# Half of a Fourier stage from the other half by symmetry, a third PSUM bank for the MLP, and two banks in turn for the first value products

## The chip, the cores and the metric

The kernel runs on one core of a Trainium2 chip. The metric is the device time of one execution in microseconds (us); the time before is the median of three runs. A profile is one execution taken by the hardware profiler. PE is TensorE, DVE is VectorE, ACT is ScalarE, POOL is GpSimd, SP is SyncE, which here only issues DMAs. SBUF is the on-chip memory, PSUM the banks that PE writes its sums into.

## The reference

Chunked attention with a few memory keys, then a Fourier mixing layer with an MLP, on 4 batches, 8 heads, 768 positions and 64 values per head (so 512 columns):

```python
for c in range(nc):                       # chunks of 32 queries
    k_full = concat([mem_k, k[l_start:r_end]])      # 8 memory keys, 16 left, 8 right of the chunk
    a = softmax(scale * q_c @ k_full.T)
    out[:, :, c_start:c_end] = a @ v_full
x = out.transpose(0, 2, 1, 3).reshape(B, S, 512)
mixed = real(fft(fft(x, axis=1), axis=2))
u = x + mixed
un = (u - mean(u)) / sqrt(var(u) + 1e-06)           # over the 512 columns
result = u + maximum(un @ w_ch1, 0) @ w_ch2         # 512 -> 2048 -> 512
```

For real x, the real part of the two-dimensional transform at position S - k and column 512 - c is that at position k and column c.

## The kernel before

Work is written as tasks (`add(engine, cost, emit, after, take, give)`) with an engine, an estimated cost, predecessors and the buffers that a task takes and gives. `Plan.order` runs a list schedule over the estimates, and the instructions are emitted in that order. On the chip, each engine works through its own list in order and waits on semaphores for the others. So a task that is late holds everything behind it on its engine.

**Attention** works on pairs of heads, n = 0 to 15, four to a batch. POOL loads q and k (`e_load_qk`, L286), SP loads v with the memory values (`e_load_v`, L295 to L304). PE turns q and k by transposes (trq and trk, L313); ACT or DVE copies them (qT, kT). PE makes the scores of six tiles of 64 queries at a time (g = 0 and 1; `e_scores`, sc, L351) into a bank of its own, ACT takes the exponential (`e_exp`, L359), and PE multiplies with the values (`e_values`, L372) into the one bank xa. DVE divides by the sums and stores the result as rows of x in SBUF (`e_norm`, L382 and L383; tile `xsb`, 6 tiles of 128 positions by 512 columns).

**Fourier stage.** DVE folds x by symmetry over columns and positions (zy, pq, ff; L400 to L417, in batch 0 by parts, L468 to L486), ACT and DVE split it into two fp16 parts (`e_hi`, `e_lo`, in batch 0 `g_hi`, `g_lo`), and PE transforms over positions (`e_rows`, ps, L440; in batch 0 `g_rows`, L534). ACT and DVE split the result into two fp16 parts (`e_up`, L452; `e_rest`, L456). par = 0 and 1 are the even and odd halves of the columns, ab = 0 and 1 the cosine and sine parts. Only 385 of the 768 positions are computed; DVE writes the mirrored ones as a reversed copy (`e_dn`, L461). Then PE transforms over columns for each of the six tiles (`e_columns`, pm, L545, eight matmuls of 256 columns): tiles 0 to 2 from up, tiles 3 to 5 from dn. DVE adds x (`e_sum`, L551) and takes mean and variance (`e_stats`), ACT subtracts the mean (`e_un`, L563). The result is transposed for the MLP, in batch 0 by PE (tp, L570, and `e_unT`), in the others by a DMA that SP issues (`e_flip`, L575).

**MLP.** For each half of a batch (three tiles): 16 times four matmuls into ph (L596), each followed by ACT's relu into hT (L603); then three tiles of 16 matmuls into pc (L610), each followed by DVE's scaling and addition (`e_osb`, L616) and ACT's output DMA (`e_out`, L620). MLP matmuls are fillers: they go where PE has nothing more urgent. Eight halves follow one another, in order of batches.

**PSUM.** Two banks `acc` hold trk (batch 0), ps and pm; two banks `mlp` hold ps for par = 1 of batch 0, tp, ph and pc; sc, tr and xa have one each. In the last batch alone every third ph or pc takes acc:

```python
def mtag(b, i):
    return "acc" if b == B - 1 and i % 3 == 2 else "mlp"
```

Up to the first ps, the plan puts matmuls on zeros (`e_fill`, L654) into PE's gaps, into one of the mlp banks.

DMAs of SP and ACT signal on eight semaphores in turn, in the order of emission; a DMA waits until the one before it on its semaphore has landed.

Of the kernel before, what the change touches and what calls it, by code (L numbers as in the profile page):

```python
# [10 lines left out]
FP32 = mybir.dt.float32  # L11
BF16 = mybir.dt.bfloat16
FP16 = mybir.dt.float16
AFT = mybir.ActivationFunctionType
ALU = mybir.AluOpType
# [16 lines left out]
def strided(src, off, dims):  # L32
    return bass.AP(tensor=src.tensor, offset=src.offset + off,
                   ap=[list(src.ap[0])] + [list(d) for d in dims])
# [105 lines left out]
def kernel(  # L140
# [51 lines left out]
    plan = Plan(dict(qs=NS, ks=NS, va=NV, kTb=NKT, qT=2, tr=1, sc=1, xa=1, e1=3,  # L192
                     xsb=3, fold=2, hl=1, up=4, dn=4, acc=2, mlp=2, un=6, unT=2, hT=1, osb=3))
    add = plan.add
# [168 lines left out]
    def e_values(n, g):  # L363
        e1 = e1_of.pop((n, g))
        xa = aps.tile([P, 3, 2, 66], FP32, tag="xa", bufs=1, name="xa")
        xa_of[n, g] = xa
        for st in range(3):
            for hh in range(2):
                v1 = va[n % NV]
                for half in range(2):  # L370
                    t6 = 2 * st + half
                    nc.tensor.matmul(xa[64 * half:64 * half + 64, st, hh, 0:65],  # L372
                                     e1[:, hh, t6, :], v1[:, hh, 6 * g + t6, 0:65],
                                     start=True, stop=True)
# [13 lines left out]

    zy_of, pq_of, ff_of, hl_of, ps_of, up_of, pm_of, un_of, tp_of = ({} for _ in range(9))
    mu_of, unT_of, rstd_of, g_of = {}, {}, {}, {}  # L390
    mid = cpool.tile([P, 2, NST, 1], FP16)
    mid32 = cpool.tile([P, NST, 1], FP32)
    warm = cpool.tile([P, 1], FP32)
    gate = cpool.tile([P, 1], FP32)

# [63 lines left out]
    def e_dn(b, par, ab):  # L459
        dn = fpool.tile([P, 2, HS], FP16, tag="dn", bufs=4, name="dn")  # L460
        nc.vector.tensor_copy(dn, rev_ap(up_of[b, par, ab][2], HS, HS, [[2 * NK, 2]]))  # L461
        up_of[b, par, ab][1] = dn

    def g_zy(par, g):
# [84 lines left out]
    def e_sum(b, kt):  # L549
        uv = xs[b][:, kt, :].rearrange("p (j c) -> p c j", c=2)  # L550
        nc.vector.tensor_tensor(uv, pm_of.pop((b, kt)), uv, ALU.add)  # L551

# [19 lines left out]
    def e_flip(b, kt):  # L572
        if kt == 0:
            unT_of[b] = fpool.tile([P, NDT, S], FP16, tag="unT", bufs=2, name="unT")
        nc.sync.dma_start_transpose(unT_of[b][:, :, ts(kt, P)], un_of.pop((b, kt)))  # L575

# [9 lines left out]


    def mtag(b, i):
        return "acc" if b == B - 1 and i % 3 == 2 else "mlp"

# [22 lines left out]
    def e_osb(b, sh, stl):  # L613
        st = sh * 3 + stl
        osb_of[b, st] = osb = fpool.tile([P, DM], FP32, tag="osb", bufs=3, name="osb")
        nc.vector.scalar_tensor_tensor(osb, pc_of.pop((b, sh, stl)), rstd_of[b][:, st:st + 1],  # L616
                                       xs[b][:, st, :], ALU.mult, ALU.add)

    def e_out(b, st):
        nc.scalar.dma_start(out[b, ts(st, P), :], osb_of.pop((b, st)))  # L620


    t_zero = add("DVE", 0.2, e_zero, rank=-21)
# [68 lines left out]
    def attention(n):  # L692
# [25 lines left out]
        for g in range(2):  # L718
            s_ = add("PE", 0.32, lambda g=g: e_scores(n, g), [eq, ek], take=("sc",),
                     give=("qT", "kTb") if g == 1 else ())  # L720
            t_sc[n, g] = s_
            x_ = add("ACT", 2.4 if (n, g) == (0, 0) else 1.12, lambda g=g: e_exp(n, g),
                     [s_, t_masks, t_after.get(n)], take=("e1",), give=("sc",))
            tag = "xa"
            v_ = add("PE", 0.85, lambda g=g: e_values(n, g), [x_, lv, t_low[n % NV]], take=(tag,),
                     rank=len(plan.tasks) + (50 if (n, g) == (2, 1) else 25) if first else None,
                     give=("e1", "va") if g == 1 else ("e1",))
            take = ("xsb",) if g == 0 and n % HP == 0 else ()
            t_norm[n, g] = add("DVE", 0.78, lambda g=g: e_norm(n, g),
                               [v_, t_norm[n - n % HP, 0] if (n % HP, g) != (0, 0) else None],  # L730
                               take=take,
                               give=(tag,))
# [61 lines left out]
    def first_fourier():  # L794
# [38 lines left out]
        return columns_of(0, t_rest)  # L833

    def fourier(b):
        nrm = [[t_norm[b * HP + i, g] for i in ii for g in range(2)] for ii in ((0, 1), (2, 3))]
        t_rest = {}
# [27 lines left out]
    def columns_of(b, t_rest):  # L865
        t_dn = {}
        for par in range(2):
            for ab in range(2):
                t_dn[par, ab] = add("DVE", 0.36, lambda par=par, ab=ab: e_dn(b, par, ab),
                                    [t_rest[par, ab]], take=("dn",))  # L870
        t_un = {}
        allr = list(t_rest.values())
        cols = {}

        def columns(kt):
            cols[kt] = add("PE", 0.9, lambda: e_columns(b, kt),
                           allr + [t_rows] + (list(t_dn.values()) if kt > 2 else []),
                           take=("acc",), rank=len(plan.tasks) + (15 if kt == 3 else 0),
                           give=("up",) * 4 if kt == 2 else ("dn",) * 4 if kt == 5 else ())

        sa = None
        columns(0)
        for kt in range(NST):
            if kt + 1 < NST:
                columns(kt + 1)
            su = add("DVE", 0.7, lambda kt=kt: e_sum(b, kt), [cols[kt]], give=("acc",))
            sa = add("DVE", 0.9, lambda kt=kt: e_stats(b, kt), [su, sa])
            un = add("ACT", 0.72, lambda kt=kt: e_un(b, kt), [sa], take=("un",))
            if b > 0:
                t_un[kt] = add("SP", 0.1, lambda kt=kt: e_flip(b, kt), [un, t_un.get(kt - 1)],  # L890
                               take=("unT",) if kt == 0 else (), give=("un",), moved=0.8,
                               loose=True)
                continue
# [9 lines left out]
    def mlp(b, t_un, rs):  # L903
        for sh in range(2):
            relu = []
            c2 = None
            for ht in range(NHT):
                ph = add("PE", 0.65, lambda sh=sh, ht=ht: e_ch1(b, sh, ht),
                         mlp_prev + [t_un[3 * sh + i] for i in range(3)] + t_w1,
                         take=(mtag(b, ht),), give=("unT",) if sh == 1 and ht == NHT - 1 else (),  # L910
# [5 lines left out]
            for stl in range(3):  # L916
                st = 3 * sh + stl
                for part in range(4):
# [6 lines left out]
                          take=("osb",),   # L925
                          give=(mtag(b, stl), "xsb") if st == NST - 1 else (mtag(b, stl),),
                          rank=RELU(len(plan.tasks)))
                mlp_prev[0] = c2
                add("ACT", 0.1, lambda st=st: e_out(b, st), [os_], give=("osb",), moved=0.9,
                    rank=RELU(len(plan.tasks)))  # L930
# [47 lines left out]
```

## Time and profile before

| | us |
|---|---|
| median of three runs (308.47 to 309.29) | 309.03 |
| the profiled execution's own time | 308.85 |
| its span, first to last instruction | 307.1 |
| PE / DVE / ACT / POOL busy | 289.5 / 171.2 / 161.5 / 40.8 |
| first matmul that is kept (trq) | 6.47 |
| first ps of batch 0 | 42.4 |
| MLP of batch 0 begins | 65.1 |
| last matmul ends | 303.15 |

The span is 1.75 us shorter than the execution's time. Matmuls overlap in PE's pipeline, so what one costs is the distance to the next one's start, not its own duration. The chain of waits is followed back from the last instruction; what it names is what the end hung on. A wait that ends on "issue" hung on nothing that the profile shows.

### The profile page before, as it was taken

What the parts mean: (1) busy time and instruction counts of PE and PEld (TensorE: products, weight loads), DVE (VectorE), ACT (ScalarE), POOL (GpSimd) and SP (SyncE); (2) the same over time, 40 slices, a digit from 0 to 9 for tenths busy, and PEclk for the clock granted to TensorE, in tenths of its full rate; (3) what the DMA queues carried; (4) which work ended last, traced back from release to release, by engine and by line L of the source; (5) the groups of instructions that cost most, each with busy time, mean ns of one, the idle gap of its engine ahead of it and who ended that gap; (6) DMA issues with size and microseconds to landing.
All of it is one profiled execution on the core that took longest, in us unless ns stands there. A gap on an engine that the chain in (4) does not pass through costs nothing.

```text
span 307.1 us, 7496 instructions
## 1 busy us (share of the span) xinstructions
PE 289.5 (94%) x3148; PEld 181.5 (59%) x3148; DVE 171.2 (56%) x371; ACT 161.5 (53%) x291; POOL 40.8 (13%) x78
## 2 busy tenths in 40 slices
PE   1399999999999999999989999999999999999994
PEld 1267678866666676666756646675554554554541
DVE  7877895975397887797764399476101001001001
ACT  6656373689884666885257423743360450531710
POOL 8806421132201102000020000000200000000000
PEclk9999999999999999999999999999999999999999
DMA  6989999999944925821361011004201101001011
GB/s 114 197 171 167 204 205 196 198 204 178 193 72 91 203 45 111 136 47 40 89 137 36 2 46 59 0 19 102 86 2 40 64 2 68 34 2 71 31 36 68
DMA packets 60289, 28.93 MB, mean 94 GB/s; under 512 B 48480, under 2 KB 56672, under 8 KB 60256
## 3 DMA queue, kind: packets, MB, share of 16 engines
q1 hardware_dynamic: 47168, 11.61, 21.0%
q0 software_dynamic: 9344, 10.49, 20.8%
q10 hardware_dynamic: 3744, 6.36, 5.7%
q8 instruction: 25, 0.41, 0.5%
q14 instruction: 8, 0.07, 0.1%
HBM read 30.28 MB, written 6.29 MB: 119 GB/s over the span
## 4 chain that ended last, share of the span: by engine, by line
PE 91%; DMA 2%; POOL 2%; DVE 1%; ACT 1%; issue 1%; POOLq 0%; ACTq 0%
PE ph L596 28%; PE pc L610 27%; PE xa L372 9%; PE pm L545 7%; PE ps L440 5%; PE idle L654 5%; PE ps L534 4%; PE sc L351 3%; DMA qs<-in_q_dram 2%; PE trk L313 2%; PE trq L313 2%; DVE osb L616 1%; POOL qs L286 0%; ACT hT L603 0%; PE tp L570 0%
## 5 line engine op out<-in xcount | busy, mean ns | idle before, releaser
L603 ACT ACTIVATE hT<-ph 128x384 f16<-128x384 f32 x128 | 60.9, 492 | 63.0 <-PE ph L596 51.5
L596 PE MATMUL ph<-unT,w_sb 128*128 128x384 f16 x512 | 91.6, 326 | 2.2 <-ACT hT L603 1.1
L610 PE MATMUL pc<-w_sb,hT 128*128 128x512 f16 x384 | 86.9, 379 | 0.0
L596 PEld LDWEIGHTS <-w_sb 128*128 128x128 f16 x512 | 47.8, 97 | 36.8 <-issue 5.7
L616 DVE SCALAR_TENSOR_TENSOR osb<-pc,rstd,xsb 128x512 f32<-128x512 f32 x24 | 18.0, 749 | 82.5 <-PE pc L610 82.4
L610 PEld LDWEIGHTS <-hT 128*128 128x128 f16 x384 | 36.8, 98 | 41.2 <-issue 0.2
L359 ACT ACTIVATE e<-sc,mbias 128x384 f32<-128x384 f32 x64 | 33.8, 583 | 13.8 <-PE sc L351 11.3
L372 PEld LDWEIGHTS xa<-va,e 128*64 128x64 f32 x768 | 25.0, 137 | 7.8 <-issue 7.0
L372 PE MATMUL xa<-va,e 128*64 128x65 f32 x768 | 29.3, 226 | 0.0
L563 ACT ACTIVATE un<-xsb,mu_s 128x512 f16<-128x512 f32 x24 | 17.2, 720 | 14.9 <-DVE mu_s L558 14.8
L382 DVE RECIPROCAL zs<-xa 128x6 f32<-128x6 f32 x32 | 6.1, 191 | 25.6 <-PE xa L372 25.5
L452 ACT CAST up<-ps 128x386 f16<-128x386 f32 x16 | 9.7, 603 | 19.1 <-PE ps L440 13.5
L551 DVE TENSOR_TENSOR xsb<-pm,xsb 128x512 f32<-128x512 f32 x24 | 16.0, 675 | 4.4 <-PE pm L545 4.2
L383 DVE TENSOR_TENSOR xsb<-xa,zs 128x384 f32<-128x384 f32 x32 | 17.8, 557 | 1.1
L557 DVE BATCH_NORM_STATS2 st<-xsb 128x6 f32<-128x512 f32 x24 | 16.4, 684 | 0.5
L654 PE MATMUL idle<-dz 128*128 128x384 bf16 x71 | 15.3, 350 | 1.0 <-DVE zero L230 1.0
L322 ACT COPY qT<-trq 128x768 bf16<-128x768 bf16 x16 | 12.8, 798 | 5.6 <-PE trq L313 5.5
L286 POOL DMA_DIRECT2D ks<-in_k_dram x16 | 10.2, 635 | 35.0 <-PE trk L313 31.4
L584 POOL TENSOR_SCALAR rstd<-mu_s 128x6 f32<-128x6 f32 x4 | 1.0, 245 | 102.0 <-DVE osb L616 57.7
L313 PE MATMUL trq<-ident_b,qs 96*64 96x96 bf16 x256 | 9.4, 221 | 5.1 <-DMA qs<-in_q_dram 5.1
L286 POOL DMA_DIRECT2D qs<-in_q_dram x16 | 10.5, 659 | 25.2 <-PE trq L313 21.5
L456 DVE TENSOR_TENSOR up<-ps,up 128x386 f16<-128x386 f32 x16 | 9.6, 598 | 7.5 <-ACT up L452 7.5
(126 smaller groups left out, 343.5 us busy)
## 6 DMA issues: line engine op xcount, KB each, us to landing
va<-in_v_dram SPq DMA_DIRECT2D x32, 220.0 KB
out_dram<-osb ACTq DMA_DIRECT2D x24, 256.0 KB
w_sb<-in_moe_w_ch_dram POOLq DMA_DIRECT2D x8, 512.0 KB, 16.9
qs<-in_q_dram POOLq DMA_DIRECT2D x16, 192.0 KB, 5.7
ks<-in_k_dram POOLq DMA_DIRECT2D x16, 192.0 KB, 6.1
va<-in_mem_v_dram SPq DMA_DIRECT2D x32, 24.0 KB
va<-in_v_dram SPq DMA_DIRECT2D x32, 22.0 KB
va<-in_v_dram SPq DMA_DIRECT2D x16, 32.0 KB
```

Source lines behind the costliest of these rows:

```text
L286: nc.gpsimd.dma_start(dst[n % NS][0:QP], src[b, 2 * pr:2 * pr + 2].rearrange("h (p j) d -> p h (j d)", j=RB))
L313: nc.tensor.transpose(out_[64 * hh:64 * hh + 64, j * w:(j + 1) * w], src[:, hh, j * D:(j + 1) * D], eye)
L359: nc.scalar.activation(e1[:, :, :, ts(half, 32)], sc[:, :, 0:6, ts(half, 32)], AFT.Exp, bias=mbias[:, half:half + 1], scale=1.0 / math.sqr ...
L372: nc.tensor.matmul(xa[64 * half:64 * half + 64, st, hh, 0:65], e1[:, hh, t6, :], v1[:, hh, 6 * g + t6, 0:65], start=True, stop=True)
L383: nc.vector.tensor_tensor(xs[b][:, 3 * g:3 * g + 3, 2 * pr * D:(2 * pr + 2) * D] .rearrange("p s (h d) -> p s h d", h=2), xa[:, :, :, 0:D] ...
L545: nc.tensor.matmul(pm[:, par, :], lhs, rhs[:, par, :], start=(im == 0), stop=(im == 3))
L563: nc.scalar.activation(un, xs[b][:, kt, :], AFT.Identity, bias=mu_of[b][:, kt, 0:1], scale=-1.0)
L596: nc.tensor.matmul(ph[:, 0:384], w1_sb[:, dt, ts(ht, P)], unT_of[b][:, dt, sh * 384:(sh + 1) * 384], start=(dt == 0), stop=(dt == NDT - 1))
L603: nc.scalar.activation(hT_of[b, sh][:, ht, :], ph_of.pop((b, sh, ht))[:, 0:384], AFT.Relu, bias=0.0, scale=-1.0)
L610: nc.tensor.matmul(pc_of[b, sh, stl], hT_of[b, sh][:, ht, ts(stl, P)], w2_sb[:, ht, :], start=(ht == 0), stop=(ht == NHT - 1))
L616: nc.vector.scalar_tensor_tensor(osb, pc_of.pop((b, sh, stl)), rstd_of[b][:, st:st + 1], xs[b][:, st, :], ALU.mult, ALU.add)
L654: nc.tensor.matmul(fill_of[0][:, 0:384], dz, strided(dz, 0, [[0, 3], [1, P]]), start=True, stop=True)
```

## The change

Three edits, in one diff.

**Mirrored sums** (batches 1 to 3). Tiles 3 to 5 get no column products of their own, and `e_dn` is left to batch 0. As soon as x is complete, SP writes its tiles 5, 4 and 3 to DRAM with the positions in reverse (`e_back`, three DMAs) and reads them back, shifted by one, as xr (`e_mirror`, four DMAs). DVE then adds the column product of tile kt (positions k), with its columns in reverse, to the mirrored x (`e_sum_back`): that gives positions 768 - k, which take the place of tile 3 + kt in xsb, with the rows in reverse. Row 0 of the first product would mirror onto itself; there PE puts position 384, by six matmuls with one weight column (`e_last_row`), once `e_sum` has read the row. Tiles are taken in the order 0, 1, 3, 4, 2, 5, so the bank of a column product is given back by `e_sum_back`. In the MLP the tiles go in the order 0, 3, 4, 5, 1, 2. Output rows of tiles 3 to 5 are reversed: SP writes them to DRAM as they are (`e_out_rows`) and then copies them within DRAM to their places (`e_out_back`).

**Third MLP bank.** `mtag` gives every third ph or pc a bank of acc in all batches.

**Two banks in turn.** In batch 0, the value products of g = 1 go to a bank of mlp (xo); g = 0 stays in xa.

```diff
-                     xsb=3, fold=2, hl=1, up=4, dn=4, acc=2, mlp=2, un=6, unT=2, hT=1, osb=3))
+                     xsb=3, fold=2, hl=1, up=4, dn=1, acc=2, mlp=2, un=6, unT=2, hT=1, osb=3))
...
-        xa = aps.tile([P, 3, 2, 66], FP32, tag="xa", bufs=1, name="xa")
+        if n < HP and g == 1:
+            xa = fps.tile([P, 3, 2, 66], FP32, tag="mlp", name="xo")
+        else:
+            xa = aps.tile([P, 3, 2, 66], FP32, tag="xa", bufs=1, name="xa")
...
+    def e_back(b):
+        for t in range(3):
+            r0 = xd[b % 2, t, 63:64, :]
+            nc.sync.dma_start(bass.AP(tensor=r0.tensor, offset=r0.offset,
+                                      ap=[[64 * DM, 2], [-DM, 64], [1, DM]]), xs[b][:, 5 - t, :])
+
+    def e_mirror(b):
+        xr_of[b] = xr = fpool.tile([P, 3, DM], FP32, tag="dn", bufs=1, name="xr")
+        xb = xd[b % 2].rearrange("t p d -> p t d")
+        nc.sync.dma_start(xr[1:65], xb[64:128])
+        nc.sync.dma_start(xr[65:128], xb[0:63])
+        nc.sync.dma_start(xr[0:1, 1:3], xb[63:64, 0:2])
+        nc.sync.dma_start(xr[0:1, 0:1], xb[63:64, 2:3])
+
+    def e_last_row(b):
+        pm = pm_of[b, 0]
+        for par in range(2):
+            todo = [(up_of[b, par, ab][0][:, part, HS:HS + 1], (cosD, nsinD)[ab])
+                    for ab in range(2 - par) for part in range(2)]
+            for i, (lhs, rhs) in enumerate(todo):
+                nc.tensor.matmul(pm[0:1, par, :], lhs, rhs[:, par, :], start=(i == 0),
+                                 stop=(i == len(todo) - 1))
+
+    def e_sum_back(b, kt):
+        pm, xr = pm_of.pop((b, kt)), xr_of[b]
+        y = xs[b][:, 3 + kt, :].rearrange("p (j c) -> p c j", c=2)
+        r = xr[:, kt, :].rearrange("p (j c) -> p c j", c=2)
+        nc.vector.tensor_tensor(y[:, :, 1:HD], strided(pm, HD - 1, [[HD - 1, 2], [-1, HD - 1]]),
+                                r[:, :, 1:HD], ALU.add)
+        nc.vector.tensor_tensor(y[:, :, 0], strided(pm, 0, [[2 * HD - 1, 2]]), r[:, :, 0],
+                                ALU.add)
...
+    SLOT = (0, 3, 4, 5, 1, 2)
...
     def mtag(b, i):
-        return "acc" if b == B - 1 and i % 3 == 2 else "mlp"
+        return "acc" if i % 3 == 2 else "mlp"
...
+    def e_out_rows(b, st):
+        nc.sync.dma_start(od[b % 2, st - 3], osb_of.pop((b, st)))
+
+    def e_out_back(b, st):
+        t = st - 3
+        p0 = 1 if t == 0 else 0
+        src, r0 = od[b % 2, t, p0:P, :], S - P * t - p0
+        top = out[b, r0:r0 + 1, :] if r0 < S else out[b, 0:1, :]
+        half = [[1, HD]]
+        nc.sync.dma_start(bass.AP(tensor=top.tensor, offset=top.offset,
+                                  ap=[[HD, 2], [-DM, P - p0]] + half),
+                          bass.AP(tensor=src.tensor, offset=src.offset,
+                                  ap=[[HD, 2], [DM, P - p0]] + half))
+        if p0:
+            nc.sync.dma_start(out[b, HS:HS + 1, :], od[b % 2, 0, 0:1, :])
...
-            tag = "xa"
+            tag = "mlp" if first and g == 1 else "xa"
...
     def fourier(b):
+        t_x1 = add("SP", 0.4, lambda: e_back(b), [t_norm[b * HP + i, 1] for i in range(HP)],
+                   moved=2.0, loose=True)
+        t_xr[b] = add("SP", 0.4, lambda: e_mirror(b), [t_x1], take=("dn",), moved=2.0, loose=True)
...
+        else:
+            kts = (0, 1, 3, 4, 2, 5)
...
+                su = add("DVE", 0.8, lambda kt=kt: e_sum_back(b, kt - 3),
+                         [cols.get(kt), t_sum[kt - 3], t_xr[b]],
+                         give=("acc", "dn") if kt == 5 else ("acc",))
```

## The prediction

> **What bounds the kernel now.** I read the page's busy times and its chain first, then TensorE's waits, the groups by form, and the timelines of the first stage and of SyncE's queue.
>
> ```profile
> span 307.1 us, 7496 instructions
> ...
> PE 289.5 (94%) x3148; PEld 181.5 (59%) x3148; DVE 171.2 (56%) x371; ACT 161.5 (53%) x291; POOL 40.8 (13%) x78
> ...
> PE 91%; DMA 2%; POOL 2%; DVE 1%; ACT 1%; issue 1%; POOLq 0%; ACTq 0%
> ```
>
> TensorE is the bound: 91% of the chain is its own work. So an instruction taken from PE shortens the run by its issue time, wherever it stands, as long as PE meets no new wait. TensorE's waits after 60 us leave little else to win:
>
> ```profile
> PE ph L596 <- ACT hT L603: 1.1, 3, 0.6
> PE ph L596 <- DVE unT L580: 0.7, 1, 0.7
> PE ph L596 <- DVE osb L616: 0.4, 2, 0.2
> ```
>
> The groups by form give the matmuls that the change touches. The 273 ns are latencies of a pipeline and not what one costs: the chain has eight of these 256-column matmuls in 0.87 us, so 0.109 us each.
>
> ```profile
> L545 PE MATMUL pm<-cosD,dn 128*128 128x256 f16 x48 | 9.2, 273 | 0.0
> L545 PE MATMUL pm<-sinD,dn 128*128 128x256 f16 x48 | 9.2, 273 | 0.0
> L534 PE MATMUL ps<-cosS,mid 128*1 128x193 f16 x18 | 2.0, 246 | 0.0
> ```
>
> **Mirrored sums, on PE.** For batches 1 to 3 the column products of tiles 3, 4 and 5 go: 3 batches x 3 tiles x 8 = 72 matmuls x 0.109 = 7.86 us. e_last_row adds 18 with a single weight column (four for par 0, two for par 1, three batches). The nearest row is cosS,mid, also one column wide: six start at 43.93 and the next group at 44.52, 0.098 us each for 193 columns. The price lies between 0.109 (the same width) and 0.098 x 256/193 = 0.130, so 1.96 to 2.34; I take 2.1. Net -5.8 us (-5.9 to -5.5).
>
> **Mirrored sums, elsewhere.** DVE loses 12 e_dn (0.36 us each) and gains 9 two-element additions (a three-element one is 0.16). e_sum_back is priced as e_sum, 0.69, plus 0.1. DVE is 56% busy, so this costs nothing while MLP matmuls keep PE fed. New is the round trip through DRAM, and SP waits in order in it: e_mirror stands behind e_back's three landings, and the later v loads, the transposes e_flip and the row outputs stand behind e_mirror. e_sum_back waits for it on DVE, and behind it there stand the next e_norm and the sums. The six matmuls of e_last_row wait for DVE's e_sum of product 0 (0.69 and signals); in PE's order a value or MLP group and product 1, 1.7 us, stand between, so this costs nothing, or up to 0.7 a batch where DVE is behind. The third column product needs a PSUM bank that only e_sum_back(3) gives back, so PE waits too.
>
> In batches 2 and 3 there is cover. In the changed order 24 and more MLP matmuls and the whole ps stage stand between the last e_norm and those sums, some 20 us of PE time by the chain's durations (in batch 3 e_mirror also stands behind an output row that waits for its osb, some 5 us). Batch 1 is tight, because SP is late there already before the change:
>
> ```profile
> 103.80 13.83 SPq L295 DMA_DIRECT2D va<-in_v_dram  x2
> 117.67 0.31 SPq L304 DMA_DIRECT2D va<-in_mem_v_dram  x1
> ```
>
> ```profile
> 114.52 0.75 DVE L616 SCALAR_TENSOR_TENSOR osb<-pc,rstd,xsb 128x512 f32<-128x512 f32 x1 [0.18 <-PE pc L610]
> ```
>
> SP stood still from 104 to 117.35 and went on when the third output tile had landed: osb ends at 115.27, so it landed 2.1 us later. SyncE's and ScalarE's DMAs take eight semaphores in turn, and one waits for the earlier one on its semaphore. In the changed program the second-last part of v before e_back(1) shares a semaphore with that same output (batch 0, tile 2).
>
> When is it out? In the changed order, PE has from the first ps to this tile's last pc: 120 ps (10.87 us in the chain) and 36 more (3.03), 12 groups of scores (0.284 each, 3.4), 12 of transposes (0.43 and 0.47, 5.4), 48 pm (5.2), 9 of values (0.853 each, 7.7), 24 tp (2.0), 64 ph (0.1645 each, 10.5) and 48 pc (0.2165 each, 10.4): 58.5 us. From 40.2 (below), with 1.15 of a new wait there and 0.9 at changes between groups (what the same sum misses in the trace of before, without the unT wait), that is 100.7. DVE is later: ps of par 0 ends near 96.9, then up 0.6, rest 0.6, two ff 2.0, a lo 0.95 behind its hi 0.8, an e_norm 0.75; so osb ends near 102.5, and the output lands at 104.9 with issue and 2.1. Five short v issues then take 2.0 us (by the rows from 117.35 and 120.89), so e_back starts at 107.0, its third issue at 108.2.
>
> A leg is bounded below by 2.05 us (the output of 93.30, 256 KB, landed by 95.35) and above by 5.9 (the median landing of a 192 KB qs load). With four issues of e_mirror in 1.8 us the rows stand in SBUF at 114.1 or at 121.8. PE comes to the third column product near 116.0 (the same sum, carried on by 14.6 us, and 0.7 for changes), and the addition and its signal take 1.05 us. So the wait is 0 or 6.85 us. I take 1.0, near the low end, since the DMA engines are 32% busy from 108 to 116 and the 5.9 belongs to loads in a full queue.
>
> The clock adds to a long wait. The trace has PE slow early and fast later, for the same 16 transposes:
>
> ```profile
> 18.73 0.88 PE L313 MATMUL trk<-turn_b,ks 100*64 100x100 bf16 x16
> ...
> 22.18 0.54 PE L313 MATMUL trk<-turn_b,ks 100*64 100x100 bf16 x16
> ```
>
> The Trainium skill (TensorE: Matmul & The Clock Gate, "What's actually happening") has a rule that speaks against this change: after an idle window of about 3.4 us the clock falls to half, until about 3.4 us of work have passed. By it, as an estimate, a wait of 6.85 us would cost some 1.7 us more; with the wait of 1.0 us that I take it adds nothing.
>
> The tail is as before: slots run 0, 3, 4, 5, 1, 2, so the last tile is stored directly. Tile 5 is done two tiles earlier (48 pc matmuls take 10.4 us, so 6.9 us), and its two legs of 2 to 3 us end before the last output does.
>
> **Two banks for the first values.** With one bank the products and e_norm alternate:
>
> ```profile
> 28.92 0.20 DVE L382 RECIPROCAL zs<-xa 128x6 f32<-128x6 f32 x1 [0.36 <-PE xa L372]
> 29.15 0.56 DVE L383 TENSOR_TENSOR xsb<-xa,zs 128x384 f32<-128x384 f32 x1
> ```
>
> ```profile
> 29.09 0.99 PE L654 MATMUL idle<-dz 128*128 128x384 bf16 x5
> 30.00 0.92 PE L372 MATMUL xa<-va,e 128*64 128x65 f32 x24
> ```
>
> The addition ends at 29.71 and the next product starts 0.29 later: 0.92 + 0.04 + 0.79 + 0.29 = 2.05 us a round. With two banks the scores' own bank sets the pace (score 0.28, exponential 1.05, signals: some 1.8 us). The last of the eight products starts at 20.90 + 7 x 1.8 = 33.5 (36.68 before), and DVE, with 2.8 us of gaps between 22 and 38 us, can follow. Behind it stand in the changed order the product itself (0.85), 28 fill matmuls (0.176 each, 4.9) and two groups of transposes (0.8), so the first ps starts near 40.2 (42.4 before). What is late next: batch 1's first score and a query transpose (0.74 us) now stand after ps. The second score must wait there for ACT's last up (0.60) and the exponential (1.05), where before it found it done at 43.3: about 1.15 us of new wait. In all -2.2 + 0.74 + 1.15 = -0.3 us, between -1.4 (the wait is covered) and +0.5 (DVE holds the first lo back).
>
> **Third MLP bank.** Only batch 3 has it before, and there the trace has no such waits. Of the 2.2 us above, the 1.1 on hT and 0.4 on osb go; counted from start to start around them it is 2.5. But acc is also the bank of ps, pm and the early trk, so an MLP product can now hold up a transform. I take -1.5, between -2.5 and 0.
>
> **Sum.** -5.8 - 0.3 - 1.5 + 1.0 = -6.6. The profiled execution took 308.85 us (span 307.1 and 1.75 around it), 0.2 below the median and inside the three runs' spread: 308.85 - 6.6 = 302.3 us.
>
> **Rivals.**
> *The banks bring nothing*: what hT no longer delays is paid at acc, and the first stage stays paced by DVE, 21.25 us busy of 26.5 there. 308.85 - 5.8 + 1.0 = 304.1. For it: acc serves four users. Against: PE's waits are seen.
> *Mirrored rows late*: both legs as the loads have them, 302.3 - 1.0 + 6.85 = 308.1; half-way 305. For it: v loads are in SP's queue just ahead. Against: 32% busy.
> *Slower*: one leg is held as one qs load was, 19.1 us from issue to landing, and the other takes 5.9. The rows stand at 108.2 + 19.1 + 1.8 + 5.9 = 135.0, and PE, behind DVE, waits 20: 302.3 - 1.0 + 20 = 321. The gain is gone from a wait of 7.6 us on, that is, from two legs of together 12.6 us. For it: nothing in the program holds PE's place for the rows, and DVE's e_norm stands behind them. Against: the load of 19.1 us shared the engines with 4 MB of weights, which are in long before.
>
> **How the numbers follow.** A measurement of this kernel tells 0.3%, 0.9 us, from no change. Forecast (wait in batch 1 under 2.5 us) 0.55; banks bring nothing 0.13; rows late 0.17, all of them faster: 0.85. Rows late to the end of their bound, with something small besides: the same, 0.04. Slower 0.11. The range starts from the good ends together (-5.9 - 1.4 - 2.5 = -9.8, so 299.0) and reaches through most of the late rows, to 307.6; that leaves out 0.15 above and a little below.
>
> **What would show it.** Right: 138 pm matmuls for 192; ps starting near 40 us; no PE wait on hT or osb over 0.3 us in batches 0 to 2; last matmul near 296.5. In batch 1, e_back issued near 107 and a PE or DVE wait of under 2.5 us at e_sum_back. Wrong: SP's e_mirror landing after 118, DVE waiting there for a DMA, or PE waiting on an acc bank.

## The result, and the profile after

The changed kernel takes 343.68 us (median of 4 runs, 343.04 to 344.59) against 309.16 (308.47 to 309.58) beside it: a ratio of 1.112, 95% interval 1.109 to 1.116. The forecast was 302.3 and its range ended at 307.6. The profiled execution took 344.59 us.

The page's first lines and the engines on its chain, as shown of before:

```profile
span 342.9 us, 7409 instructions
...
PE 286.5 (84%) x3086; PEld 177.7 (52%) x3086; DVE 168.7 (49%) x368; ACT 163.0 (48%) x291; POOL 40.8 (12%) x78
...
PE 67%; DMA 20%; DVE 8%; issue 2%; SPq 1%; ACT 1%; ACTq 0%; DVEq 0%
```

PE issues 62 instructions fewer (138 pm for 192, as forecast, and fewer fill matmuls), but TensorE has gone from 91% of the chain to 67%, and DMAs from 2% to 20%. TensorE's waits, in all, times and longest:

```profile
PE pm L584 <- DVE xsb L500: 30.3, 2, 20.9
PE ph L640 <- ACT hT L647: 4.3, 3, 2.4
...
PE ph L640 <- DMA unT<-un: 2.3, 1, 2.3
...
PE sc L351 <- ACT e L359: 0.8, 1, 0.8
```

Before, no wait behind 60 us was over 0.7 us. The large one is the third column product, which needs the bank that e_sum_back(3) gives back, and that sum waits on DVE for the rows:

```profile
DVE xsb L498 <- DMA xr<-x_rows: 31.5, 2, 21.7
```

The chain through batch 1 (start, duration, what):

```profile
108.77 19.54 DMA x_rows<-xsb
...
130.35 5.59 DMA xr<-x_rows
...
136.06 0.69 DVE xsb L498
...
136.87 1.89 PE pm L584 x8
```

SyncE issued the copy on time; then the write leg (three copies of 256 KB, from the third issue to the last landing) took 19.5 us and the read leg 5.6. Batch 2 repeats it:

```profile
172.44 16.69 DMA x_rows<-xsb
...
191.12 4.36 DMA xr<-x_rows
```

The clock follows the waits (window: length, PE busy, PEld, DVE, ACT and POOL busy, granted clock, DMA share, GB/s):

```profile
114.40:136.80 22.40, 1.53 (x14) 0.70 (x8) 0.74 (x2) 2.58 (x5) 0.63 (x1) 0.59 0.45 92
...
136.87:142.28 5.41, 5.41 (x44) 3.24 (x45) 5.17 (x13) 1.94 (x3) 0.63 (x1) 0.50 0.78 137
196.50:200.31 3.81, 3.23 (x13) 1.81 (x13) 3.66 (x8) 1.35 (x3) 0.00 (x0) 0.50 0.18 34
251.51:254.92 3.41, 3.41 (x12) 1.59 (x12) 0.00 (x0) 2.22 (x5) 1.46 (x2) 0.50 0.26 80
```

In the wait of batch 1 the granted clock is 0.59 on average, and behind the two waits at the sums the first 5.4 and 3.8 us run at half of it: 2.7 and 1.9 us lost. The third window stands behind the wait of 2.4 us for relu and loses 1.7, so 6.3 together. And at the end of the chain:

```profile
332.70 6.33 DMA out_dram<-osb
...
339.15 0.75 DVE osb L660
```

The last matmul ends at 335.3, but the last osb waits for one of three buffers, whose output lands 6.3 us after its issue; before, the output priced in the prediction landed in 2.05, and the last osb began 0.03 us behind PE. SyncE's queue has a mirrored output issued just ahead of it:

```profile
331.32 0.60 SPq L675 DMA_DIRECT2D out_dram<-out_rows  x1
```

From the last matmul to the end of the span it is 7.6 us, before 4.0.

A version without any copy, run below, takes 302.31 us. From there to 343.68 are 41.4 us. The waits at the sums are 30.3, the half clock 6.3, the end 3.6, the waits for relu and for a transposed tile 6.6: 46.8, which is 5.4 more than the difference, so these terms do not simply add up. They name where PE stood still; the runs show what made it stand.

### The profile page after: what moved, and what is told of

Same layout as the page of the kernel before. It is cut to its first block, busy times and chain, and to the rows that moved or that the text cites. A ratio compares the mean times of both kernels' runs of the same rounds, so it can differ in the third digit from the quotient of the medians.

```text
span 342.9 us, 7409 instructions
## 1 busy us (share of the span) xinstructions
PE 286.5 (84%) x3086; PEld 177.7 (52%) x3086; DVE 168.7 (49%) x368; ACT 163.0 (48%) x291; POOL 40.8 (12%) x78
## 3 DMA queue, kind: packets, MB, share of 16 engines
q0 software_dynamic: 9344, 10.49, 19.2%
## 4 chain that ended last, share of the span: by engine, by line
PE 67%; DMA 20%; DVE 8%; issue 2%; SPq 1%; ACT 1%; ACTq 0%; DVEq 0%
PE ph L640 22%; PE pc L654 21%; DMA x_rows<-xsb 11%; DMA out_dram<-osb 6%; PE xa L375 5%; PE idle L713 4%; PE ps L445 3%; PE ps L573 3%; PE pm L584 3%; DMA xr<-x_rows 3%; PE sc L351 2%; PE trk L313 2%; PE trq L313 2%; DVE osb L660 2%; PE xo L375 1%
## 5 line engine op out<-in xcount | busy, mean ns | idle before, releaser
L640 PE MATMUL ph<-unT,w_sb 128*128 128x384 f16 x512 | 92.8, 335 | 6.6 <-ACT hT L647 4.3
L640 PEld LDWEIGHTS <-w_sb 128*128 128x128 f16 x512 | 49.5, 100 | 42.1 <-issue 9.0
L584 PE MATMUL pm<-cosD,up 128*128 128x256 f16 x48 | 10.1, 296 | 30.3 <-DVE xsb L500 30.3
L584 PEld LDWEIGHTS <-up 128*128 128x128 f16 x96 | 9.7, 105 | 33.2 <-DVE xsb L500 21.3
L375 PE MATMUL xa<-va,e 128*64 128x65 f32 x672 | 25.7, 226 | 0.0
L375 PEld LDWEIGHTS xa<-va,e 128*64 128x64 f32 x672 | 21.9, 137 | 6.1 <-issue 4.4
L498 DVE TENSOR_TENSOR xsb<-pm,xr 128x510 f32<-128x510 f32 x9 | 6.0, 672 | 31.6 <-DMA xr<-x_rows 31.5
L386 DVE TENSOR_TENSOR xsb<-xa,zs 128x384 f32<-128x384 f32 x28 | 15.6, 557 | 1.0
L430 ACT CAST hi<-ff 128x768 f16<-128x768 f32 x12 | 9.9, 833 | 11.5 <-DVE ff L422 11.3
L385 DVE RECIPROCAL zs<-xa 128x6 f32<-128x6 f32 x28 | 5.3, 188 | 19.8 <-PE xa L375 19.6
```

The lines of the kernel that those rows point to most:

```text
L386: nc.vector.tensor_tensor(xs[b][:, 3 * g:3 * g + 3, 2 * pr * D:(2 * pr + 2) * D] .rearrange("p s (h d) -> p s h d", h=2), xa[:, :, :, 0:D] ...
L584: nc.tensor.matmul(pm[:, par, :], lhs, rhs[:, par, :], start=(im == 0), stop=(im == 3))
L640: nc.tensor.matmul(ph[:, 0:384], w1_sb[:, dt, ts(ht, P)], unT_of[b][:, dt, sh * 384:(sh + 1) * 384], start=(dt == 0), stop=(dt == NDT - 1))
```

## The experiments

Each number is the median; ratios are to the kernel before, measured beside each run (309.5 to 309.8 us throughout).

**1. How many DMA engines a copy uses.** In the trace of after, the three copies of batch 1 show as 384 packets of 2,048 bytes, 93 ns each on average, between 108.8 and 128.0 us. Their times add up to 35.7 us in these 19.2, so about two ran at a time. On two engines that is 192 x 93 ns = 17.8 us each; on sixteen, by the same 93 ns, an estimated 2.2. The Trainium skill (DMA: Bandwidth & Descriptors, "Why a DMA increments its semaphore by 16 and not by 1") says that a DMA is spread over the largest number of engines, up to 16, that divides the slowest dimension of both its patterns, counting from the lowest-numbered engine. The copy's pattern in memory is 2 x 64 x 512: two. The packets of this trace agree with two.

Theory A is that rule. Theory C: rows written in descending order are slow in themselves. The first run writes rows forward in one pattern of 128, the second forward in two groups of 64 with a row's gap, so on two engines.

```diff
-  ap=[[64 * DM, 2], [-DM, 64], [1, DM]]
+  [[DM, 128], [1, DM]]                      # e1_straight_back
+  ap=[[65 * DM, 2], [DM, 64], [1, DM]]      # e2_forward_two
```

> The changed kernel, with e_back writing its rows forward in one run of 128 (the reversal of x is left out, so the second half is added to the wrong rows of x; same bytes, same number of DMAs). Theory A (the pattern 2 x 64 x 512 is moved by two DMA engines only, so three such writes take some 18 us): the writes take 2 to 4 us, TensorE's waits of 20.9 and 9.3 us at the third column product and the half-speed stretches after them (some 3.4 us) go, the copies within DRAM still hold the outputs: 343.7 - 30.3 - 3.4 = 310, between 306 and 314. Theory B (a write to DRAM and a read of it is slow as such): still over 335. Theory D (the PSUM banks lose the time): still over 335.

> The changed kernel, with e_back writing forward, but in two halves of 64 rows with a gap of one row between them, so that the pattern is again 2 x 64 x 512 (the reversal of x is left out). Theory A (two engines): as slow as the changed kernel, 341 to 346, writes of 16 to 20 us. Theory C (rows in descending order are slow as such): as fast as the kernel with straight writes, near 310.

Measured: 317.5 us (1.025 of before) and 343.96 (1.110). The write leg fell to 4.9 us in the first and stayed at 19.6 in the second: the order of the rows costs nothing, the number of groups slows the leg, as theory A has it. But 317.5 is 7.5 above the 310 that A expected, and outside its range. One more run has the outputs straight as well:

```diff
-  ap=[[HD, 2], [-DM, P - p0]] + half        # e_out_back: two halves of each row, 127 or 128 rows
+  [[DM, 128], [1, DM]]; 127 rows as 112 and 15   # e3_both_straight
```

> The changed kernel with e_back forward in one run of 128 rows and e_out_back copying whole rows forward (127 rows as 112 and 15), so that the reversal of x and of the outputs is left out. Theory A: both long transfers are spread over the engines, no wait for a returned output buffer and no late last output: 310 - 4 - 6 = 300, between 298 and 304; what was forecast (302.3) comes out. Theory B: over 330.

Measured: 312.0 us (1.008, 1.004 to 1.011); one row of each 768 isn't put out in it. The outputs' two engines thus cost 5.5 us, but theory A alone, at 298 to 304, misses: 8 us and more are left with every copy on many engines. Its chain:

```profile
110.76 5.05 DMA x_rows<-xsb
...
116.56 8.07 DMA xr<-x_rows
```

Its SyncE queue came to the copy at 109.9, and one wait of PE at the sums of 8.4 us remains, while DMA engines are full from 118 us on with loads of v issued just behind the read.

The same with everything computed: 8 groups of 16 in place of 2 of 64.

```diff
-  ap=[[64 * DM, 2], [-DM, 64], [1, DM]]
+  ap=[[16 * DM, 8], [-DM, 16], [1, DM]]
-  xr[1:65] <- xb[64:128]; xr[65:128] <- xb[0:63]
+  for m in range(8): xr[1 + 16 * m:][:n] <- xb[112 - 16 * m:][:n]    # n = 16, at last 15
```

> The kernel after with one thing changed: the rows are turned round in 8 groups of 16 instead of 2 of 64 (and read back in eight pieces of 16 rows instead of two of 64 and 63); everything is computed, all in SyncE's queue and the bank edits in place. Theory A (spread over engines): the write leg falls from 19.5 and 16.7 us to 5 to 8 us, the sums hold PE 6 to 12 us in batch 1 (8.4 us with straight rows, and 6 more reads to issue, some 3 us), and the time is 317 to 325 us, since the outputs keep their two engines (317.5 us was the run with straight copies and these outputs). If the spread is not the cause: above 335 us.

Measured: 322.7 us (1.044), as expected. From its chain:

```profile
109.17 6.94 DMA x_rows<-xsb
...
116.25 3.82 DMA xr<-x_rows
```

So the three copies take 19.5 us on two engines, 6.9 on eight, 4.9 to 5.1 on sixteen; beside them ran the last packets of a load of v and one or two loads of q or k. The kernel goes from 343.7 to 322.7.

**2. What the copies hold up that never reads them.** The first attempt took the sums' read of xr away and left the copies; the sums then took their own rows. It was compared with TensorE's side alone, without any copy.

```diff
-  r = xr[:, kt, :]...          # e_sum_back
+  r = y
-  t_x1 = add("SP", ...); t_xr[b] = add("SP", ...)     # e14_sums_only; e18_unread keeps both
-  if b and st > 2:             # outputs straight in both, both bank edits undone
+  if False:
```

> Only TensorE's side of the mirrored sums: 72 column products fewer and 18 one-column products more, both bank edits undone, no copy through memory; the sums of the mirrored tiles take their own rows (wrong rows: that part of the computation is changed) and the outputs go straight to their place. The prediction took this side at -5.8 us. Theory S (that size was right, and all of the loss is in the copies and what waits for them): 302.5 to 304.5 us, and no wait of PE over 1 us behind 100 us. Theory O (the shorter stage only brings the flips and loads of the other queues nearer, and PE waits for them instead): 306 to 310 us, with a wait of ph for the transposed tile of 2 us or more.

> The kernel of the run just described with the copies of the kernel after issued as there (written rows first in two halves, then read), but no sum reads or waits for them. Theory W (only the sums' own wait costs time): within 1 us of that run. Theory L (the DMAs of SyncE's and ScalarE's queues take eight semaphores in turn in the order of the program, and each waits until the one eight places before it has landed, so that loads of v, outputs and transposes stand behind copies that nobody reads): 5 to 15 us above that run, with waits of SyncE's queue at the loads of v for the copies of 10 us or more and a wait of PE for transposed tiles or values.

Measured: 305.51 us (0.986, 0.983 to 0.990) and 343.22. The first is near S, a little short: -4.2 us, not -5.8, with one wait of 1.8 us for a transposed tile. The second doesn't tell W from L: the sums write in place, over the rows that the copy is still reading, so they waited for it all the same (16.1 us at most). I repeated it with copies out of the weights' tile, which nothing overwrites:

```diff
-  xs[b][:, 5 - t, :]
+  w1_sb[:, t, 0:2 * DM]       # fp16, the same bytes and pattern
```

> As the run with unread copies, but the copies take their rows from the weights' tile, which nothing overwrites: the same patterns (two halves of 64 rows of 2 KB), issues and places in the queue, and neither the sums nor anything else reads what they write or writes what they read (that part of the computation is left out; outputs go straight). TensorE's side alone was 305.5 us, the run whose sums still waited for the copy 343.2. Theory W (the sums' wait for the copy is the loss): 305 to 309 us, no wait of PE pm for the sums. Theory L (loads of v, outputs and transposes stand behind copies through the eight semaphores): 312 to 325 us, and PE waits for transposed tiles, q, k or values.

Measured: 333.97 us. Nothing waits for the data of these copies, and still they cost 28.5 us over the run without them, more than L expected. One of its chains, behind batch 2's copy:

```profile
163.51 17.89 DMA x_rows<-w_sb
...
183.91 4.42 DMA unT<-un
...
188.41 0.72 ACT un L599
189.13 0.39 ACT hT L644
...
189.56 2.71 PE ph L637 x8
```

SyncE stands at the read until the copy has landed; behind it stands a transpose of batch 1, ACT waits for the buffer that the transpose frees, and PE waits for ACT (2.1 us here). The longest wait of this run, 11.4 us, comes on the same way from the transpose before it, which is issued directly behind the copies. The queue shows there, and at the copies of batch 1, a second coupling:

```profile
107.36 6.03 SPq L471 DMA_DIRECT2D x_rows<-w_sb  x3
113.49 6.62 SPq L299 DMA_DIRECT2D va<-in_v_dram  x1
...
168.34 7.25 SPq L611 DMA_TRANSPOSE unT<-un  x1
```

A load of v, issued in 0.59 us elsewhere, takes 6.62 to issue behind the copies, and a transpose 7.25 in place of 1.22. The three issues of the copies themselves take 5.2 us on two engines in the kernel after, 2.1 on eight and 1.5 on sixteen. So a DMA that sits on two engines also slows down what its queue issues next; that the shared engines' queues are full there is a reading of these lines, which no run isolates.

**3. Another queue.** If what is left is the place in SyncE's queue, the copies should go elsewhere: in the run with all copies straight, the rows of batch 1 are complete at 85.6 us, and SyncE comes to them at 109.9. First the straight copies, then the 8 groups, from ScalarE's queue; then the groups from GpSimd's (with the value products' bank, without the third feed-forward bank).

```diff
-  nc.sync.dma_start(...)       # e_back, e_mirror
+  nc.scalar.dma_start(...)     # e12_act, e13_groups_act
+  nc.gpsimd.dma_start(...)     # e19_pool
```

> The run with all copies in one straight pattern (rows are not turned round, so the sums take wrong rows: that part of the computation is changed; 312.0 us), with the copies for the mirrored sums issued from ScalarE's queue instead of SyncE's, and the planner told of legs of 6.0 and 8.7 us. In that run the rows of batch 1 were complete at 85.6 us and SyncE issued the copy at 109.9 us, for it stood behind two loads of v, one of which waited 15.6 us for the transfer of an output; the sums then held PE 8.4 us. Theory Q (what is left of the loss is the place in SyncE's queue): the copy is issued at 86 to 90 us, the wait of PE pm for the sums goes (under 1 us), and the time falls by 8.4 us and by some 1.7 us of half clock behind the wait, to 301 to 304 us. Theory R (the engines of the DMA are full with loads of v, or ScalarE pays for the issues with 3.5 us a batch): the wait moves to another place and the time stays at 309 to 313 us.

> A version that computes everything: the kernel after, with the rows turned round in 8 groups of 16 rows (the groups are put in order by eight reads of 16 rows each) and these copies issued from ScalarE's queue; the outputs' own turning round stays as in the kernel after (two halves of a row's columns, 127 or 128 packets of 1 KB on each of 2 engines). Theory A (the write leg is set by the number of engines that its pattern spreads over): the write leg of 384 packets of 2 KB on 8 engines is 48 x 93 ns = 4.5 us alone, 5 to 8 us with the loads beside it, and PE's wait for the sums of 20.9 and 9.3 us is gone; with outputs that still land 5 to 6 us after their issue, 306 to 312 us, that is 305 to 307 plus what the outputs hold at the end. If the number of engines is not the cause, the leg stays near 17 to 20 us; it then ends at 107 us, still before PE needs the rows at 114 us, so look at the leg and not at the time.

> A version that computes everything: mirrored sums with the value products' bank (third feed-forward bank undone), the rows turned round in 8 groups of 16 and these copies issued from GpSimd's queue, whose DMAs don't share the semaphores of SyncE's and ScalarE's; the outputs' own turning round as in the kernel after. Theory L: without shared semaphores no load of v and no transpose waits for a copy; the rows are there before PE needs them at 114 us and the time is 302 to 308 us, the upper end from outputs that still take 5 to 6 us on two engines at the end of the kernel. Theory N (GpSimd's own DMAs cost more: 13 issues a batch in line with its loads of q and k): scores wait for q or k, and the time is 312 us or more.

Measured: 316.69, 325.72 and 308.71 us (the last with ratio 0.998, 0.994 to 1.003). On ScalarE the copy went out at 85.5 us, the wait at the sums was gone, and the time rose. The wait had moved, as theory R has it, but to a place that R does not name; the time is 4 us over R's range, and e13 misses its own by 14. In e12's chain:

```profile
140.85 6.17 DMA xr<-x_rows
...
147.08 1.21 SPq L612
...
151.86 3.67 DMA unT<-un
...
155.58 1.46 PE ph L638 x4
```

SyncE's transpose (L612) waits for ScalarE's read of xr, whose semaphore the program gives it in turn. Behind it stand loads of v and then the transpose that PE waits for, 13.6 us. Loads of v wait for ScalarE's copies too:

```profile
SPq L295 <- DMA x_rows<-xsb: 33.9, 2, 20.8
```

GpSimd's DMAs have semaphores of their own; in e19 neither SyncE nor ScalarE waits for x_rows or xr, PE has no wait over 2 us behind 20 us, and its last matmul ends at 299.2, 3.9 us earlier than before. (The third feed-forward bank is undone there as well, so the 14 us from e8 to e19 are not the queue's alone.) The time is still 0.7 above theory L's range, for the kernel gives the gain back at the end, where the last osb waits until 303.1:

```profile
296.53 6.43 DMA out_dram<-osb
```

That is a plain output, issued 1.3 us behind a mirrored one. I tried to clear this: mirrored tiles first in the last batch (e20), then five output buffers for three (e22), and, apart from these, mirrored sums in batches 1 and 2 alone (e24).

```diff
+  LAST = (3, 4, 5, 0, 1, 2)                      # e20_last_order
-  tag="osb", bufs=3
+  tag="osb", bufs=5                              # e22_osb5
+  plain = b in (0, B - 1)                        # e24_two_batches: batch 3 as before
```

> The version with the copies on GpSimd's queue, with the mirrored tiles of the last batch put first in its feed-forward (tiles 3, 4, 5, 0, 1, 2 instead of 0, 3, 4, 5, 1, 2); it computes everything. In that version PE ended at 295.7 us, but the last sum waited until 303.1 us for a buffer whose output landed 6.4 us after its issue, beside a mirrored output on the same two engines. Theory T (the tail is that collision): the last output is then issued beside none of them and the kernel ends some 4 us after PE, as TensorE's side alone did (299.7 to 303.7): 301 to 304 us. Theory U (outputs land late anyhow, because of the number of bytes): 306 to 309 us.

> The version just described with five output buffers instead of three, so that no sum waits for an output that is still under way (DVE's waits for that were 11.9 us in two). Theory T: 301 to 303.5 us, PE without the wait of 1.5 us at 258 us. Theory U: the last output still lands 6 us after its issue; 304 to 307 us.

> The version with the copies on GpSimd's queue (groups of 16, value products' bank, two feed-forward banks), with the mirrored sums in batches 1 and 2 alone; batch 3 computes all six of its tiles and puts out all of them directly, as in the kernel before. It computes everything. Theory T (what holds that version is the last batch's mirrored outputs): TensorE's side gives two thirds of the 4.2 us that it gave alone, the value products' bank 2.0 us as it did alone, so 309.6 - 2.8 - 2.0 = 304.8 us (303.5 to 306.5). Theory U (the outputs of batch 2, or GpSimd's copies, hold it): 307 to 311 us.

Measured: 310.30, 318.71 and 308.85 us, all three as late as theory U had it or later; that the number of bytes is the reason is not shown. (The 295.7 us that e20's expectation gives for PE's end is the end of the second-last tile; the last matmul of e19 ended at 299.2.) In e20 the last osb follows the last matmul at once, but PE gets there only at 303.5, with an output of 5.5 us ahead and six waits for relu of 0.6 us in the last batch. In e22 PE ends at 299.8 and the span 18.4 us behind it; SyncE's row outputs wait 16.2 us, in three waits, for ScalarE's. In e24 a mirrored output of batch 2 leaves SyncE at 273.45, and the plain one behind it is late again:

```profile
274.78 6.25 DMA out_dram<-osb
```

**4. The bank edits.** Together, each alone, and the change without them.

```diff
 # e4_banks: before + both; e5_bank3: before + mtag; e6_xo: before + xo; e17_no_banks: after - both
```

> The kernel before with the two bank edits alone (third MLP bank in all batches, value products of g = 1 of the first batch in a bank of mlp), nothing mirrored. By the prediction's terms: 309.1 - 0.3 - 1.5 = 307.3, between 305 and 309.6. Theory D (the banks lose the time): over 312.

> Kernel before with one edit of the change alone: the feed-forward products of batches 0 to 2 use a third PSUM bank, as those of batch 3 did before. The prediction took this edit at -1.5 us (-2.5 to 0). The run with both bank edits and nothing else stood at 1.0073 of before, that is 2.3 us slower, with PE held for 3.8 us by one late DMA transpose and the granted clock at 0.7 to 0.8 in two slices behind that wait. Theory P (the planner's order: a third bank lets the products run ahead, so that the order of the other queues moves, and the third transpose of batch 1 stands behind loads of v): this edit alone is slower, 311 to 313 us, and the wait of ph for the transposed tile of 3 to 4 us is in its trace. Theory X (the loss belongs to the value products of batch 0): 306.5 to 308.5 us, no such wait.

> Kernel before with the other bank edit alone: in batch 0 the value products of the second half of each pair go to a bank of the feed-forward. The prediction took it at -0.3 us (first row products at 40.2 against 42.4 us, less a wait of 1.15 us at the second score). Theory P (the loss of the two bank edits comes with the third bank): 308.3 to 309.5 us, within 0.3% of before, with the wait of sc for e of 0.8 us and no wait for a transposed tile. Theory X: 311 to 313 us.

> The kernel after with both bank edits undone: the mirrored sums alone, complete. The two bank edits alone stood at +2.3 us, the third bank alone at 0.0 (with a wide scatter, 307.0 to 312.9), the value products' bank alone at -2.0. Theory A (the legs on two DMA engines set the time): 340 to 347 us, with the wait of PE for the sums of 18 us or more in batch 1, no more than 3 us from the kernel after. If the bank edits were the larger part: below 330 us.

Measured: 311.98 (1.007, 1.005 to 1.010); 310.36, spread from 307.0 to 312.9 over 12 runs (1.000, 0.997 to 1.003); 307.33 (0.993, 0.991 to 0.996); 361.42. Alone, the value products' bank gains 2.2 us beside its kernel before, more than either theory had it, and the third bank nothing. The third bank's runs part by the granted clock: the four at 1.0 took 307.0 to 308.3 us, the eight at 0.986 to 0.994 took 309.8 to 312.9. Together the two edits lose 2.5, a miss of the forecast (305 to 309.6) that stays just under theory D's 312:

```profile
146.04 2.02 DMA out_dram<-osb
...
148.12 0.32 SPq L295
...
149.37 2.45 DMA unT<-un
...
151.87 1.46 PE ph L599 x4
```

In the reordered queue the third transpose of batch 1 stands behind a load of v, and this on an output's semaphore. PE waits 3.8 us, and the clock behind it is 0.50 for 5.7 us (an estimate of 2.8 us lost). Theory P's wait is there in the pair; the third bank alone has one of 2.9 us, but not theory P's time. In the kernel after, the banks help: without them it is 17.7 us slower, with 39.3 us of waits at the sums (21.9 in batch 1, 17.4 in batch 2). I had expected at most 3; why the cover shrinks that much was not looked into further.

Last, TensorE's side with the value products' bank, without copies:

```diff
 # e14_sums_only + xo
```

> TensorE's side of the mirrored sums with the value products' bank: no copy, sums of the mirrored tiles on their own rows (wrong rows: that part of the computation is changed), outputs straight. If the two gains add, 309.6 - 4.2 - 2.0 = 303.4 us (302.5 to 304.5); if the order of the other queues takes it back, 305 to 308 us with a wait of PE for transposed tiles of 2 us or more.

Measured: 302.31 us (0.976, 0.974 to 0.979). The two gains add, 309.5 - 4.2 - 2.2 = 303.1 and 0.8 more. No wait of PE over 1 us is left behind 20 us. It is the bound for this change, and its rows are wrong; of the versions that compute everything, e6_xo, the one edit without the mirrored sums, is the fastest at 307.33 us and beats both kernels.

## Why the prediction was wrong, point by point

*The failed step* is the bound on a leg, "below by 2.05 us" and "above by 5.9". Both rows belong to a single transfer that does not run on two engines (and for the load of q the profile's page has 5.7, not 5.9). The write leg is three transfers of 256 KB, and its pattern runs on two: it took 19.5 and 16.7 us, where the same three take 4.9 to 5.1 on sixteen engines (experiment 1). Both patterns stood in the diff, and so did the rule for reading them in the Trainium skill (DMA: Bandwidth & Descriptors, the section named in experiment 1); I priced the bytes of one transfer, not the patterns of three. With the measured times in the step's sum: third issue at 108.8, 19.5, reads 2.0, 5.6, so rows at 135.9, against PE's need at 115 to 116: the 20.9 us that PE waited. And the wait of 1.0 that I took, near the low end, would have failed on sixteen engines too: with every copy straight PE still waited 8.4 us at the sums, above the 6.85 of the upper bound, while loads of v filled the DMA engines behind the read.

*"In batches 2 and 3 there is cover, some 20 us"*: in batch 2, legs of 16.7 and 4.4 us with their issues (172.4 to 195.5) used it up, and PE waited 9.4 us. Batch 3 held.

*"Its two legs of 2 to 3 us end before the last output does"*: failed by the same mis-sizing. The legs within DRAM have patterns for two engines too, and plain outputs beside them land after 4.8 to 6.4 us. It cost 3.6 us at the end; in e3, where these legs are straight as well, the last osb follows the last matmul at once.

*"The clock adds to a long wait"*: the mechanism was right. The estimate of 1.7 us for one wait, from the Trainium skill (TensorE: Matmul & The Clock Gate, "What's actually happening"), compares with 2.7 and 1.9 lost in windows at 0.50; the 5.4 us at half clock in batch 1 are longer than the page's 3.4. It was set to nothing because the wait itself was taken as 1.0.

*Not priced at all*: what stands behind the copies besides the sums. The text named the v loads, transposes and row outputs in SyncE's queue, but gave them no time. Experiment 2 puts 28.5 us on them when the sums' own wait is gone. This is why the sums' wait and the queue's are not two terms to add: with the one removed, the other holds PE.

*Mirrored sums on PE, -5.8*: direction right, size -4.2 alone, where a new wait of 1.8 us for a transposed tile covers the rest. Beside the value products' bank, where no such wait is left, it is -5.0 (307.33 to 302.31).

*Two banks, -0.3*: the first ps at 40.0 (40.2 forecast) and the new wait at the second score (0.8 us for about 1.15) were right; the gain alone was 2.2. With this edit alone, the first ps comes 1.9 us earlier than before, the first MLP product 2.1 and the last matmul 1.9: what I added for the moved score and the wait was not paid on the way to the end.

*Third bank, -1.5*: alone nothing over all its runs. The 1.1 us on hT and 0.4 on osb do go from its trace, but a wait of 2.9 us for a transposed tile came in their place. The profiled run kept the full clock behind that wait and took 307.0 us, so the forecast gain is there; that the other runs lost it to half clock behind this wait fits their lower granted clock, but is not shown, for none of them was profiled.

*e_back's start*: 107.0 forecast, 107.56 measured:

```profile
107.56 5.21 SPq L474 DMA_DIRECT2D x_rows<-xsb  x3
```

*The rival "slower"* had batch 1 right (a wait of 20 us, 321 us) from a row with another cause, a load of 19.1 us beside 4 MB of weights. With batch 2's 9.4, the half clock's 6.3 and the end's 3.6 it would have been 340.3. Its chance of 0.11 was too low because the mechanism that it named was a rare accident, where the real one came in every batch.

## What to carry to other kernels

Price a DMA by its pattern before its bytes: read off the slowest dimension on both sides, ask how many engines that gives, and take the duration from a row of the same shape, for all the transfers of the leg together. A transfer that is added to a queue must also be priced for everything behind it in that queue and on its semaphores, even if its own reader can wait; moved to another queue that shares the semaphores, it took its wait along. And a run meant to remove a wait has to remove every dependence of that kind: here the overwriting of the copy's source kept it alive.

## What the runs showed of the hardware that I had not expected

The same three transfers of 256 KB took 19.5, 6.9 and 4.9 us on two, eight and sixteen engines, beside loads of the same kinds. A plain output took 6.3 us in place of 2.05 when a copy within DRAM on two engines was issued just ahead of it. And short waits of TensorE can cost clock, but not always: 2.4 us idle were followed by 3.4 us at half clock (the kernel after), 3.8 us by 5.7 (both banks), while 1.8 us (e14) and 2.9 us (the third bank's profiled run) left the clock at 1.0.
